# Batches in every eighth row of a quadrant, one transfer for the rows, and merged VectorE copies

## The chip, the cores and the metric

The kernel runs on one core of a Trainium2 chip. The metric is the device time of one execution in microseconds, as the median of several runs. TensorE, VectorE, ScalarE and GpSimd compute; SyncE issues nearly all transfers between HBM and the on-chip memory, which sixteen transfer engines carry out.

## The reference

One decoding step for four sequences (B = 4, one token each, D = 448): pre-LayerNorm, attention over the last 1024 positions of a cache with 16 query heads in 8 groups (head size 256), a residual, and then an MLP behind two further LayerNorms (D to 1792, GELU, back to 448) with biases and a residual. All in float32.

```python
def _A_ref(x, k_cache, v_cache, wq, wo):
    W = min(4096, max(256, Sk // 4))              # 1024
    q = (x @ wq).reshape(B, Sq, 16, 256).transpose(0, 2, 1, 3)
    k = repeat(k_cache[:, :, Sk - W:, :], 2, axis=1)
    v = repeat(v_cache[:, :, Sk - W:, :], 2, axis=1)
    p = softmax(einsum("bhqd,bhkd->bhqk", q, k) * 256 ** -0.5)
    return einsum("bhqk,bhkd->bhqd", p, v).transpose(0, 2, 1, 3).reshape(B, Sq, 4096) @ wo

def _B_ref(x, w1, b1, w2, b2):
    return gelu(layernorm(x) @ w1 + b1) @ w2 + b2

h = x + _A_ref(layernorm(x), k_cache, v_cache, wq, wo)
out = h + _B_ref(layernorm(h), w1, b1, w2, b2)
```

## The kernel before

The 128 partitions are used as four quadrants of Q = 32. In the attention a quadrant is a batch element, and the two query heads of a group are two of its 32 rows. Outside it, a quadrant is a fourth of the columns of x, and the four batch elements are four of its rows, the first four (rows 0 to 3, 32 to 35 and so on). TensorE works on four quadrants side by side: a matmul takes weights of 32 columns (or fewer, where only some rows are wanted) and writes to the partitions of its quadrant.

SyncE loads everything in an order written out by hand: `wq0` with x transposed, `k0`, two small pieces of `wq1`, and then in turn a block of k (with the projection weights of the next group but one) and a block of v (with its part of wo), 4992 KB each for most of the eight groups, two buffers for k and two for v (`load`, L48 to L54, all issued from L52). At the end v7 comes in four pieces, then `w1` in two and `w2` in three, in the buffers of k. The biases and rows of x come as `rows`, in four transfers of four rows on ScalarE's queue, one for each quadrant (L132), into the tile `rs`, which GpSimd clears first.

Each group g goes through `project_q` (L156: a projection, four transposes, a sum over the quadrants `sm`, two copies into `qT`), `scores` (L175: 32 matmul instructions, the row maximum `mx`, `nm` = -maximum x scale in two VectorE operations, the exponential), `transpose_p` (L203: eight transposes, four copies into `pT`), `values` (L216) and `transposed_output` with `add_output` (L234, L246). The scores of group g + 1 stand ahead of the values of group g. The order on TensorE is fixed as written (a manual schedule); the other engines' order is that of the scheduler.

After the last group comes a tail: group 7's output goes into `last`, the residual and the two LayerNorms follow (`h`, `d`, `z` and their sums through matmuls with `fold`), `z` is transposed by a matmul with `rows_of`, a selection of columns of the identity, into `zT`; `pu` (L388) multiplies it with w1, GELU gives `u`, which is transposed by `rows_of` (`put`, L407, L409) into `gT` (L411 on VectorE, L414 on ScalarE), and w2 is applied in two parts: `pa` (L421, chunks 0 to 7, copied out as `pas`) and `py` (L431, chunks 8 to 13, with `pas` added by L256). The sum with `hb` is stored as 128 rows of 512 bytes (L438). `keep_warm` issues matmuls without use for the clock. In `pu`, `pa` and `py` the first matmul of an accumulation takes weights of 32 columns, the others of four:

```python
m = Q if a == 0 else B
```

Of the kernel before, what the change touches and what calls it, by code (L numbers as in the profile page):

```python
# [11 lines left out]
ALU = mybir.AluOpType  # L12
# [3 lines left out]
B, D = 4, 448  # L16
HQ, HKV, SK, DH = 16, 8, 4096, 256
REP = HQ // HKV
W = min(4096, max(256, SK // 4))
F = 1792  # L20
P = 128
H = P // 2
ND = 4
NKC = W // P
NFC = F // P
FQ = F // 4
Q = 32
CACHE = NKC * B * DH
WEIGHTS = 4 * D
EPS = 1e-5  # L30
SCALE = DH ** -0.5

@with_exitstack
def block_kernel(ctx: ExitStack, tc, rows, wq0, k0, wq1, kq, vo, w1, w2, out):
    nc = tc.nc
# [30 lines left out]
    def load_k(g):  # L66
        half = CACHE // 2
        if g == 0:
# [3 lines left out]
            for i in range(2):  # L72
                nc.sync.dma_start(
                    wq1_last[i * Q : (i + 1) * Q, :], wq1[i].rearrange("e (p c) -> e p c", c=512)[:, :4, :]
                )
# [18 lines left out]
    ident = const.tile([P, P], F32, name="ident")  # L94
# [5 lines left out]

    sel = const.tile([P, Q], F32, name="sel")
    nc.vector.tensor_add(sel, ident[:, 0:Q], ident[:, Q : 2 * Q])
    nc.vector.tensor_add(sel, sel, ident[:, 2 * Q : 3 * Q])
    nc.vector.tensor_add(sel, sel, ident[:, 3 * Q : 4 * Q])


    yT = const.tile([P, ND + 1, Q], F32, name="yT")
    nc.vector.memset(yT, 0.0)
    wq1_last = const.tile([H, 512], F32, name="wq1_last")
    zT = const.tile([P, ND, Q], F32, name="zT")  # L110
# [5 lines left out]
        nc.vector.tensor_scalar_mul(fold[: 3 * Q, j, :], sel[: 3 * Q, :], 1.0 / D)  # L116
        nc.vector.tensor_scalar_mul(fold[3 * Q :, j, :], sel[3 * Q :, :], 0.5 / D)
    fold = fold.rearrange("p j q -> p (j q)")
    rows_of = ident.rearrange("p (j q) -> p j q", j=4)[:, :, :B]
    qT = [const.tile([P, 2, B, Q], F32, name=f"qT{i}") for i in range(2)]  # L120
    pT = [const.tile([P, NKC // 2, B, Q], F32, name=f"pT{i}") for i in range(2)]
    oT = [const.tile([P, 4, Q], F32, name=f"oT{i}") for i in range(2)]
    gT = const.tile([P, NFC, Q], F32, name="gT")
# [4 lines left out]

    rs = const.tile([P, 2 * P + FQ], F32, name="rs")
    nc.gpsimd.memset(rs, 0.0)  # L130
    for j in range(4):
        nc.scalar.dma_start(rs[j * Q : j * Q + B, :], rows[j])  # L132
    xb, b2b, b1b = rs[:, :P], rs[:, P : 2 * P], rs[:, 2 * P :]


# [20 lines left out]
    def project_q(g, parts):  # L156
        pq = ps_m.tile([P, 512], F32, tag="m", name=f"pq{g}")
        for j, y, cols, w in parts:
            nc.tensor.matmul(pq[j * Q : (j + 1) * Q, cols], y, w, start=True, stop=True)  # L159
        qs = work.tile([P, 512], F32, tag="qs", name=f"qs{g}")  # L160
        nc.scalar.copy(qs, pq)  # L161

        pt = ps_m.tile([P, 2 * REP, P], F32, tag="m", name=f"pqt{g}")
        for i in range(2 * REP):
            nc.tensor.transpose(pt[:, i, :], qs[:, i * P : (i + 1) * P], ident)  # L165
        sm = work.tile([P, 2 * REP, B], F32, tag="sm", name=f"sm{g}")
        nc.vector.tensor_reduce(  # L167
            sm, pt.rearrange("p i (j q) -> p i q j", j=4)[:, :, :B, :], axis=AX.X, op=ALU.add
        )

        src = sm.rearrange("p (r c) b -> p c b r", r=REP)
        for i in range(2):
            nc.vector.tensor_copy(qT[g % 2][:, :, :, i * REP : (i + 1) * REP], src)

    def scores(g, kt):  # L175
        mx = work.tile([P, 2], F32, tag="mx", name=f"mx{g}")
        halves = []
        for h in range(2):
            s = ps_s.tile([P, 512], F32, tag="s", name=f"s{g}_{h}")
            for c in range(2):  # L180
                for b in range(B):
                    nc.tensor.matmul(  # L182
                        s[b * Q : (b + 1) * Q, :], qT[g % 2][:, c, b, :], kt[h][:, c, b, :],
                        start=(c == 0), stop=(c == 1),
                    )
            nc.vector.reduce_max(mx[:, h : h + 1], s, axis=AX.X)  # L186
            halves.append(s)
        nm = work.tile([P, 1], F32, tag="nm", name=f"nm{g}")
        nc.vector.tensor_max(nm, mx[:, 0:1], mx[:, 1:2])
        nc.vector.tensor_scalar_mul(nm, nm, -SCALE)  # L190
        p = work.tile([P, 2 * 512], F32, tag="p", name=f"p{g}")
        sums = work.tile([P, 2], F32, tag="sums", name=f"sums{g}")
        for h in range(2):
            nc.scalar.activation(  # L194
                p[:, h * 512 : (h + 1) * 512], halves[h], AF.Exp, bias=nm, scale=SCALE,
                accum_out=sums[:, h : h + 1],
            )
        rec = work.tile([P, 1], F32, tag="rec", name=f"rec{g}")
        nc.vector.tensor_add(rec, sums[:, 0:1], sums[:, 1:2])
        nc.vector.reciprocal(rec, rec)  # L200
        return p, rec

    def transpose_p(g, p):  # L203
        for h in range(2):
            pt = ps_t.tile([P, 4, P], F32, tag="t", name=f"ppt{g}_{h}")
            for c in range(4):
                nc.tensor.transpose(pt[:, c, :], p[:, (4 * h + c) * P : (4 * h + c + 1) * P], ident)  # L207

            src = pt.rearrange("p (c i) (b q) -> p c i b q", i=2, b=B)
            for i in range(2):  # L210
                nc.vector.tensor_copy(  # L211
                    pT[g % 2][:, 2 * h : 2 * h + 2, :, i * REP : (i + 1) * REP], src[:, :, i, :, :REP]
                )


    def values(g, vt, po, pairs=range(NKC // 2)):  # L216
# [17 lines left out]
    def transposed_output(g, po, rec):  # L234
        o = work.tile([P, 2, DH], F32, tag="o", name=f"o{g}")
        nc.vector.tensor_scalar_mul(o, po, rec)  # L236
        pt = ps_m.tile([P, 2, 2, P], F32, tag="m", name=f"pot{g}")
        for i in range(2):
            for c in range(2):
                nc.tensor.transpose(pt[:, i, c], o[:, i, c * P : (c + 1) * P], ident)  # L240
        dst = oT[g % 2].rearrange("p (r c) q -> p c r q", r=REP)[:, :, :, :B]
        src = pt.rearrange("p i c (b q) -> p i c q b", b=B)
        nc.vector.tensor_copy(dst, src[:, 0, :, :REP])  # L243
        nc.vector.tensor_add(dst, dst, src[:, 1, :, REP : 2 * REP])  # L244
# [32 lines left out]
    p, rec = scores(0, kt)  # L277
    project_q(1, wqt)
    transpose_p(0, p)
    for g in range(HKV - 2):  # L280
        kt, wqt = load_k(g + 1)
        vt, wot = load_v(g)
        p, rec_next = scores(g + 1, kt)
# [9 lines left out]
    g = HKV - 2  # L293
# [5 lines left out]
    t = load("k", w2, (8 * D, 4 * D, 2 * D), "w2")  # L299
    w2t = [t[:, c * D : (c + 1) * D] for c in range(NFC)]  # L300
    p, rec_last = scores(g + 1, kt)


# [29 lines left out]
    for i in range(4):  # L333
        for j in range(4):
            nc.tensor.matmul(
                ph[j * Q : (j + 1) * Q], oT[(g + 1) % 2][:, i, :], columns(wo_last[:, i, :], j),
                start=False, stop=(i == 3),
# [18 lines left out]
    h = once.tile([P, P], F32, tag="h", name="h")  # L356
# [3 lines left out]
    m = row_mean(hs, pm[:, 0:1], "m")  # L360
# [4 lines left out]
    m = row_mean(ds, pm2[:, 0:1], "m2")  # L365
# [5 lines left out]
    nc.scalar.activation(junk, z, AF.Square, accum_out=zv)  # L371
    pz = ps_m.tile([P, 4, B], F32, tag="m", name="pz")
    nc.tensor.matmul(pz, z, rows_of, start=True, stop=True)
    nc.vector.tensor_copy(zT[:, :, :B], pz)
    hb = once.tile([P, P], F32, tag="hb", name="hb")
    nc.vector.tensor_add(hb, h, b2b)
    keep_warm(1, warm)
# [4 lines left out]
    pu = ps_s.tile([P, 512], F32, tag="s", name="pu")[:, :FQ]  # L382
    pv = ps_m.tile([P, 2], F32, tag="m", name="pv")
    for a in range(ND):
        m = Q if a == 0 else B
        for j in range(4):
            rows, w = w1_part(a, j)
            nc.tensor.matmul(  # L388
                pu[j * Q : j * Q + m, :], zT[rows, a, :m], w, start=(a == 0), stop=(a == ND - 1),
            )  # L390
        if a == 0:
            rsqrt(r1, row_mean(dv, pv[:, 0:1], "v1"), "r1")
        if a == 1:
            v2 = stat("v2")
            nc.vector.tensor_scalar(v2, row_mean(zv, pv[:, 1:2], "v2"), r1, r1, op0=ALU.mult, op1=ALU.mult)
            rsqrt(s, v2, "r2")
            nc.vector.tensor_mul(s, s, r1)
# [7 lines left out]
    put = ps_m.tile([P, 4, 4, B], F32, tag="m", name="put")  # L405
# [2 lines left out]
    for rows in (slice(0, H), slice(H, P)):  # L408
        nc.tensor.matmul(put[rows, 3], u[:, 3 * P :], rows_of, start=True, stop=True)  # L409
    dst = gT[:, :12, :].rearrange("p (c j) q -> p c j q", c=3)  # L410
    nc.vector.tensor_copy(dst[:, :, :, :B], put[:, :3])  # L411

    for i, rows in enumerate((slice(0, H), slice(H, P))):
        nc.scalar.copy(gT[rows, 12:, :B], put[rows, 3].rearrange("p (j i) q -> p j i q", i=2)[:, :, i, :])  # L414
    keep_warm(1, warm)

    first = 8
    pa = ps_w.tile([P, D], F32, tag="acc", name="pa")
    for c in range(first):
        j, m = c % 4, Q if c < 4 else B  # L420
        nc.tensor.matmul(  # L421
            pa[j * Q : j * Q + m, :], gT[:, c, :m], w2t[c], start=(c < 4), stop=(c >= first - 4),
        )
    pas = once.tile([P, D], F32, tag="u", name="pas")
    nc.scalar.copy(pas, pa)
    py = ps_o.tile([P, 2, H], F32, tag="o", name="py")
    for c in range(first, NFC):
        for j in range(4):
            m, n = (Q, 2) if c == first else (B, 2 if j < 3 else 1)
            w = columns(w2t[c], j) if n == 2 else w2t[c][:, None, 3 * P :]  # L430
            nc.tensor.matmul(  # L431
                py[j * Q : j * Q + m, :n, :], gT[:, c, :m], w, start=(c == first), stop=(c == NFC - 1),
            )
        if c == first + 1:
            add_quadrants(py, pas, False)
# [69 lines left out]
```

## Time and profile before

| | before |
|---|---|
| median of 3 runs | 214.59 us (214.52 to 214.6) |
| profiled execution, first to last instruction | 212.9 us |
| median less that span | 1.7 us |
| TensorE busy | 137.9 us (65%), 971 matmul instructions |
| VectorE busy | 39.2 us (18%), 167 instructions |
| ScalarE busy | 21.0 us (10%), 52 instructions |
| moved by transfers | 88.46 MB, 415 GB/s over the span |

The span is that of one profiled execution, which has no other time of its own; the difference to the median lies outside the first and the last instruction. Busy time says how long an engine worked, not whether anyone waited for it. A transfer is spread over several of the sixteen transfer engines and is complete when the slowest of them is.

### The profile page before, as it was taken

To read this page: it belongs to the slowest core of one execution; us is meant where nothing else is said; L and a number is where in the kernel's file an instruction comes from. 1 tells how busy PE (TensorE), PEld (TensorE's weight loads), DVE (VectorE), ACT (ScalarE), POOL (GpSimd) and SP (SyncE) were. 2 spreads that over 40 slices of the span, in tenths; PEclk is the share of its full clock that TensorE was granted. 3 is DMA by queue.
4 is the path that set the end of the run, shared out by engine and by line. 5 is a ranking of instruction groups with operands and counts; after the bars stand their busy time and mean duration, and the time that the engine had idled before them with its cause. 6 is when DMAs were issued, how large, how long until landed. Compare 5 with 4: busy or idle time off the path is not lost.

```text
span 212.9 us, 2306 instructions
## 1 busy us (share of the span) xinstructions
PE 137.9 (65%) x971; PEld 49.1 (23%) x971; DVE 39.2 (18%) x167; ACT 21.0 (10%) x52; POOL 5.6 (3%) x17
## 2 busy tenths in 40 slices
PE   0456868093886739583986348382948476798994
PEld 0322233021231212211231113120222123234432
DVE  1420324001130202210130104110230231022320
ACT  0210213000030000300030003000030001000311
POOL 6100000000000000000000000000000000000110
PEclk9999999669597966969599859979797999699999
DMA  7999998999989999999999999999989999999991
GB/s 291 426 399 469 398 465 378 459 465 390 458 378 465 465 390 458 398 446 465 390 458 405 443 465 386 465 413 428 461 375 468 440 428 390 417 418 433 424 390 60
DMA packets 3865, 88.46 MB, mean 415 GB/s; under 512 B 448, under 2 KB 576, under 8 KB 1168
## 3 DMA queue, kind: packets, MB, share of 16 engines
q1 hardware_dynamic: 3824, 88.29, 96.9%
q8 instruction: 7, 0.11, 0.2%
q10 hardware_dynamic: 32, 0.05, 0.1%
q14 instruction: 2, 0.02, 0.0%
HBM read 88.26 MB, written 0.07 MB: 415 GB/s over the span
## 4 chain that ended last, share of the span: by engine, by line
DMA 85%; PE 11%; DVE 2%; issue 0%; SPq 0%
DMA v<-vo 65%; DMA w<-w 12%; DMA k<-k 8%; PE po L219 8%; PE acc L248 1%; DVE o L236 1%; PE pot L240 1%; PE py L431 1%; DVE oT L243 0%; DVE oT L244 0%; SPq L52 0%; DVE res L437 0%; PE py L256 0%
## 5 line engine op out<-in xcount | busy, mean ns | idle before, releaser
L182 PE MATMUL s<-k,qT 128*32 128x512 f32 x256 | 42.3, 822 | 24.7 <-DMA k<-kq 22.6
L219 PE MATMUL po<-v,pT 128*32 128x512 f32 x256 | 40.0, 772 | 19.6 <-DMA v<-vo 19.6
L186 DVE TENSOR_REDUCE mx<-s 128x1 f32<-128x512 f32 x16 | 11.1, 691 | 67.4 <-PE s L182 67.4
L182 PEld LDWEIGHTS s<-k,qT 128*32 128x32 f32 x256 | 10.0, 146 | 54.7 <-issue 29.4
L219 PEld LDWEIGHTS po<-v,pT 128*32 128x32 f32 x256 | 10.7, 135 | 42.3 <-issue 31.4
L161 ACT COPY qs<-pq 128x512 f32<-128x512 f32 x8 | 4.7, 586 | 135.8 <-PE pq L159 135.8
L236 DVE TENSOR_SCALAR o<-po,rec 128x512 f32<-128x512 f32 x8 | 6.0, 750 | 60.2 <-PE po L219 60.2
L194 ACT ACTIVATE p<-s,nm 128x512 f32<-128x512 f32 x16 | 10.9, 690 | 18.4 <-DVE nm L190 18.4
L207 PE MATMUL ppt<-ident,p 128*128 128x128 f32 x64 | 10.5, 286 | 2.0 <-ACT p L194 1.7
L165 PE MATMUL pqt<-ident,qs 128*128 128x128 f32 x32 | 5.7, 304 | 6.2 <-ACT qs L161 6.2
L240 PE MATMUL pot<-ident,o 128*128 128x128 f32 x32 | 5.2, 286 | 5.7 <-DVE o L236 5.7
L248 PE MATMUL acc<-v,oT 128*32 128x448 f32 x56 | 6.7, 551 | 3.3 <-DVE oT L244 3.3
L207 PEld LDWEIGHTS ppt<-ident,p 128*128 128x128 f32 x64 | 6.7, 140 | 6.0 <-ACT p L194 6.0
L159 PE MATMUL pq<-k,yT 128*32 128x512 f32 (+1 forms) x66 | 7.3, 515 | 0.0
L308 PE MATMUL warm<-idle 128*32 128x512 bf16 x25 | 7.3, 382 | 0.0
L240 PEld LDWEIGHTS pot<-ident,o 128*128 128x128 f32 x32 | 3.3, 140 | 13.0 <-DVE o L236 13.0
L165 PEld LDWEIGHTS pqt<-ident,qs 128*128 128x128 f32 x32 | 3.6, 150 | 10.9 <-ACT qs L161 9.1
L153 POOL TENSOR_TENSOR r<-ve_r,mhalf 128x1 f32<-128x1 f32 x2 | 1.1, 544 | 191.9 <-DVE ve_r L152 191.9
L211 DVE COPY pT<-ppt 128x16 f32<-128x16 f32 x32 | 4.7, 170 | 4.7 <-PE ppt L207 4.7
L159 PEld LDWEIGHTS pq<-k,yT 128*32 128x32 f32 x66 | 3.1, 110 | 6.1 <-issue 4.8
L138 PE MATMUL pm_x<-wq,mean 128*128 128x12 f32 x2 | 0.6, 363 | 5.8 <-DMA wq<-wq 5.8
L167 DVE TENSOR_REDUCE sm<-pqt 128x16 f32<-128x64 f32 x8 | 1.8, 225 | 13.0 <-PE pqt L165 13.0
(101 smaller groups left out, 60.9 us busy)
## 6 DMA issues: line engine op xcount, KB each, us to landing
v<-vo SPq DMA_DIRECT2D x7, 4992.0 KB, 31.8
k<-kq SPq DMA_DIRECT2D x6, 4992.0 KB, 32.0
k<-k SPq DMA_DIRECT2D x1, 4864.0 KB, 16.3
k<-kq SPq DMA_DIRECT2D x1, 4096.0 KB
w<-w SPq DMA_DIRECT2D x2, 1792.0 KB
v<-vo SPq DMA_DIRECT2D x2, 1024.0 KB, 22.2
v<-vo SPq DMA_DIRECT2D x1, 2048.0 KB
w<-w SPq DMA_DIRECT2D x1, 1344.0 KB
```

The lines of the kernel that those rows point to most:

```text
L159: nc.tensor.matmul(pq[j * Q : (j + 1) * Q, cols], y, w, start=True, stop=True)
L161: nc.scalar.copy(qs, pq)
L165: nc.tensor.transpose(pt[:, i, :], qs[:, i * P : (i + 1) * P], ident)
L182: nc.tensor.matmul(s[b * Q : (b + 1) * Q, :], qT[g % 2][:, c, b, :], kt[h][:, c, b, :], start=(c == 0), stop=(c == 1),)
L186: nc.vector.reduce_max(mx[:, h : h + 1], s, axis=AX.X)
L194: nc.scalar.activation(p[:, h * 512 : (h + 1) * 512], halves[h], AF.Exp, bias=nm, scale=SCALE, accum_out=sums[:, h : h + 1],)
L207: nc.tensor.transpose(pt[:, c, :], p[:, (4 * h + c) * P : (4 * h + c + 1) * P], ident)
L219: nc.tensor.matmul(po[b * Q : (b + 1) * Q], pT[g % 2][:, c, b, :], vt[c][:, :, b, :], start=(c == 0), stop=(c == NKC // 2 - 1),)
L236: nc.vector.tensor_scalar_mul(o, po, rec)
L240: nc.tensor.transpose(pt[:, i, c], o[:, i, c * P : (c + 1) * P], ident)
L248: nc.tensor.matmul(acc[i * Q : (i + 1) * Q, :], oT[g % 2][:, i, :], wt[:, i, :], start=(g == 0), stop=(g == HKV - 2),)
L308: nc.tensor.matmul(warm[:Q], idle[:, :Q], idle, start=True, stop=True)
```

## The change

A batch element's row in a quadrant is now every eighth one (rows 0, 8, 16, 24 of 32; STEP = Q // B = 8) instead of the first four. So the sixteen rows of x and of the biases lie at partitions 0, 8, ..., 120, and one transfer of sixteen rows brings them. `rows_of` picks every eighth column of the identity; `oT`, `zT` and `gT` are written with a step of eight, and the matmuls of `pu`, `pa` and `py` take weights of 32 columns throughout, so that their outputs fill whole quadrants. The store itself has the same shape as before; the host picks other rows of it.

Apart from that, pairs of VectorE operations become single ones: the two copies into `qT` (8 fewer), two of the four copies into `pT` (16 fewer), and the two operations of `nm` (8 fewer), 32 in all.

```diff
-    rows_of = ident.rearrange("p (j q) -> p j q", j=4)[:, :, :B]
+    rows_of = ident.rearrange("p (j q) -> p j q", j=4)[:, :, ::STEP]
...
-    for j in range(4):
-        nc.scalar.dma_start(rs[j * Q : j * Q + B, :], rows[j])
+    nc.scalar.dma_start(rs[::STEP, :], rows)
...
-        src = sm.rearrange("p (r c) b -> p c b r", r=REP)
-        for i in range(2):
-            nc.vector.tensor_copy(qT[g % 2][:, :, :, i * REP : (i + 1) * REP], src)
+        src = sm.rearrange("p (r c) b -> p c b r", r=REP)[:, :, :, None, :].to_broadcast([P, 2, B, 2, REP])
+        nc.vector.tensor_copy(qT[g % 2][:, :, :, : 2 * REP].rearrange("p c b (i r) -> p c b i r", i=2), src)
...
-        nc.vector.tensor_max(nm, mx[:, 0:1], mx[:, 1:2])
-        nc.vector.tensor_scalar_mul(nm, nm, -SCALE)
+        nc.vector.tensor_scalar(nm, mx[:, 0:1], mx[:, 1:2], -SCALE, op0=ALU.max, op1=ALU.mult)
...
-            src = pt.rearrange("p (c i) (b q) -> p c i b q", i=2, b=B)
-            for i in range(2):
-                nc.vector.tensor_copy(
-                    pT[g % 2][:, 2 * h : 2 * h + 2, :, i * REP : (i + 1) * REP], src[:, :, i, :, :REP]
-                )
+            src = pt.rearrange("p (c i) (b q) -> p c b i q", i=2, b=B)[:, :, :, :, :REP]
+            dst = pT[g % 2][:, 2 * h : 2 * h + 2, :, : 2 * REP]
+            nc.vector.tensor_copy(dst.rearrange("p c b (i r) -> p c b i r", i=2), src)
...
-        dst = oT[g % 2].rearrange("p (r c) q -> p c r q", r=REP)[:, :, :, :B]
+        dst = oT[g % 2].rearrange("p (r c) q -> p c r q", r=REP)[:, :, :, ::STEP]
...
-    nc.vector.tensor_copy(zT[:, :, :B], pz)
+    nc.vector.tensor_copy(zT[:, :, ::STEP], pz)
...
-        m = Q if a == 0 else B
...
-                pu[j * Q : j * Q + m, :], zT[rows, a, :m], w, start=(a == 0), stop=(a == ND - 1),
+                pu[j * Q : (j + 1) * Q, :], zT[rows, a, :], w, start=(a == 0), stop=(a == ND - 1),
...
-            pa[j * Q : j * Q + m, :], gT[:, c, :m], w2t[c], start=(c < 4), stop=(c >= first - 4),
+            pa[j * Q : (j + 1) * Q, :], gT[:, c, :], w2t[c], start=(c < 4), stop=(c >= first - 4),
...
-            m, n = (Q, 2) if c == first else (B, 2 if j < 3 else 1)
+            n = 2 if c == first or j < 3 else 1
...
-                py[j * Q : j * Q + m, :n, :], gT[:, c, :m], w, start=(c == first), stop=(c == NFC - 1),
+                py[j * Q : (j + 1) * Q, :n, :], gT[:, c, :], w, start=(c == first), stop=(c == NFC - 1),
```

The writes of `gT` (L411, L414) get the step of eight in the same way.

More of the change, by code (lines that the diff above doesn't have):

```diff
@@ L27 @@
 Q = 32
+STEP = Q // B
 CACHE = NKC * B * DH
@@ L410, in block_kernel @@
     dst = gT[:, :12, :].rearrange("p (c j) q -> p c j q", c=3)
-    nc.vector.tensor_copy(dst[:, :, :, :B], put[:, :3])
+    nc.vector.tensor_copy(dst[:, :, :, ::STEP], put[:, :3])
     for i, rows in enumerate((slice(0, H), slice(H, P))):
-        nc.scalar.copy(gT[rows, 12:, :B], put[rows, 3].rearrange("p (j i) q -> p j i q", i=2)[:, :, i, :])
+        nc.scalar.copy(gT[rows, 12:, ::STEP], put[rows, 3].rearrange("p (j i) q -> p j i q", i=2)[:, :, i, :])
     keep_warm(1, warm)
@@ L419, in block_kernel @@
     for c in range(first):
-        j, m = c % 4, Q if c < 4 else B
+        j = c % 4
         nc.tensor.matmul(
-            pa[j * Q : j * Q + m, :], gT[:, c, :m], w2t[c], start=(c < 4), stop=(c >= first - 4),
+            pa[j * Q : (j + 1) * Q, :], gT[:, c, :], w2t[c], start=(c < 4), stop=(c >= first - 4),
         )
@@ L488 @@
     rows = np.concatenate([quadrants(xp), quadrants(b2), quadrants(np.asarray(B_b1).reshape(1, F))], axis=2)
+    rows = rows.reshape(4 * B, 2 * P + FQ)
     arrays = {
@@ L502 @@
     r = run(nc, [arrays], core_ids=[0])
-    got = np.asarray(r.results[0]["out"]).reshape(4, Q, P)[:, :B, :]
+    got = np.asarray(r.results[0]["out"]).reshape(4, B, STEP, P)[:, :, 0]
     return np.ascontiguousarray(got.transpose(1, 0, 2).reshape(B, 1, 4 * P)[:, :, :D])
```

## The prediction

> **What bounds the kernel now.** I read the page's header and slices first, then its queues and its chain. Columns of a queue row: packets, MB, time of those packets as a share of what 16 transfer engines have in the span.
>
> ```profile
> span 212.9 us, 2306 instructions
> DMA  7999998999989999999999999999989999999991
> ...
> q1 hardware_dynamic: 3824, 88.29, 96.9%
> q8 instruction: 7, 0.11, 0.2%
> q10 hardware_dynamic: 32, 0.05, 0.1%
> ...
> HBM read 88.26 MB, written 0.07 MB: 415 GB/s over the span
> ```
>
> SyncE's queue (q1) fills 96.9% of the engines' time, and no slice between the first and the last falls under 80%. 88.29 MB have to pass, so the end of the stream sets the end unless something starves it. Two views say whether anything can: the issues (KB each, median us from issue to landing) and what SyncE waited for (us, times, longest).
>
> ```profile
> v<-vo SPq DMA_DIRECT2D x7, 4992.0 KB, 31.8
> k<-kq SPq DMA_DIRECT2D x6, 4992.0 KB, 32.0
> ...
> rs<-rows ACTq DMA_DIRECT2D x4, 11.0 KB
> ```
> ```profile
> SPq L52 <- PE acc L248: 48.7, 6, 8.5
> SPq L52 <- PE pq L159: 39.0, 6, 7.5
> ...
> SPq L52 <- DMA k<-k: 11.4, 1, 11.4
> ```
>
> A block of 4992 KB takes 4992 x 1024 B / 415 GB/s = 12.3 us, but it lands 32 us after its issue: 32 - 12.3, about 20 us of it, is queueing behind earlier blocks. SyncE's waits for a free buffer (`acc`, `pq`) last at most 8.5 us and end with those 20 us still queued. An earlier release changes an issue time, not a transfer. The chain on the page, which alternates transfers with TensorE's work, follows buffer releases and hides this.
>
> The second place is the end: the timeline (start, us busy, what, [idle before <-releaser]) and the stretches (us, PE busy (x), PEld, DVE, ACT, POOL, PEclk, DMA share, GB/s).
>
> ```profile
> 207.49 0.55 PE L421 MATMUL pa<-w,gT 128*4 128x448 f32 x3
> 208.15 0.53 ACT L425 COPY pas<-pa 128x448 f32<-128x448 f32 x1 [1.62 <-PE pa L421]
> ...
> 208.41 0.64 PE L431 MATMUL py<-w,gT 128*32 128x128 f32 x16 [0.37 <-DMA w<-w]
> ...
> 208.78 0.48 PE L256 MATMUL py<-pas,sel 128*32 128x128 f32 x8
> ...
> 209.00 1.14 PE L431 MATMUL py<-w,gT 128*4 128x64 f32 x32
> 210.21 0.29 DVE L437 TENSOR_TENSOR res<-py,hb 128x128 f32<-128x128 f32 x1 [4.05 <-PE py L431]
> ```
> ```profile
> 206.50:207.00 0.50, 0.50 (x8) 0.13 (x4) 0.00 (x0) 0.03 (x1) 0.00 (x0) 1.00 0.92 380
> 207.00:207.50 0.50, 0.50 (x12) 0.13 (x4) 0.00 (x0) 0.00 (x0) 0.00 (x0) 1.00 0.75 308
> 207.50:208.00 0.50, 0.50 (x8) 0.00 (x0) 0.00 (x0) 0.00 (x0) 0.00 (x0) 1.00 0.61 244
> 208.00:208.50 0.50, 0.13 (x7) 0.09 (x8) 0.00 (x0) 0.35 (x1) 0.00 (x0) 1.00 0.60 244
> 208.50:209.00 0.50, 0.50 (x24) 0.50 (x28) 0.00 (x0) 0.18 (x1) 0.00 (x0) 1.00 0.17 65
> ```
>
> TensorE is done with `pa` at 207.49 + 0.55 = 208.04, waits 0.37 us for a piece of w2, and then works without a gap to 210.14. The end has two covers: 0.37 us in front of `py`, and between the end of `pas` (208.15 + 0.53 = 208.68) and L256, which reads it (208.78), 0.10 us. And the transfer engines do not end together: from 207.5 to 208.5 the share is 0.60, ten of sixteen at work, six finished a full us earlier. A load counts as landed when the slowest engine is through, so what matters is which engines carry more.
>
> **The change part by part.** The 32 VectorE instructions:
>
> ```profile
> L211 DVE COPY pT<-ppt 128x16 f32<-128x16 f32 x32 | 4.7, 170 | 4.7 <-PE ppt L207 4.7
> ...
> L173 DVE COPY qT<-sm 128x16 f32<-128x16 f32 x16 | 2.0, 172 | 0.3
> ...
> L189 DVE TENSOR_TENSOR nm<-mx 128x1 f32<-128x1 f32 x8 | 1.3, 159 | 0.3
> ...
> L190 DVE TENSOR_SCALAR nm<-nm 128x1 f32<-128x1 f32 x8 | 1.2, 154 | 0.3
> ...
> L411 DVE COPY gT<-put 128x48 f32<-128x48 f32 x1 | 0.2, 208 | 1.3 <-PE put L409 1.3
> ...
> L374 DVE COPY zT<-pz 128x16 f32<-128x16 f32 x1 | 0.2, 175 | 0.5 <-PE pz L373 0.5
> ```
>
> A pair of copies of 16 elements (2 x 170 ns) becomes one of 32. Its price lies between 172 (16 elements) and 208 ns (48), so I take 190: 16 in `transpose_p` save 16 x (340 - 190) = 2.4 us, 8 in `project_q` 8 x (344 - 190) = 1.2, and the 8 of `nm` 8 x about 0.15 = 1.2. That makes 4.8 us of VectorE. All of it lies in the eight groups before the last `v` block; nothing in the tail is merged. The cover is the 20 us queue, and SyncE's release comes from `pq` and `acc`, which stand before the merged copies or on a chain (L236, L243, L244) that keeps its instructions. Worth 0. With the cover gone it would be 4.8 / 8 = 0.6 us a group.
>
> Writing every eighth row: `qT` and `pT` are already written in runs of two values, and those copies take 170 and 172 ns against 175 for `zT`, which is written in runs of four. Single values should cost the same, bounds -5 to +10 ns on five operations of the tail (two on `oT`, one on `zT`, one on `gT`, the pair on ScalarE): +0.02 us, hidden by the covers. `rows_of` as a moving operand with a step of eight has no row before it; eight matmuls of 16 columns read it. If each cost as much as 128 columns instead of 16, that is 273 - 266 ns:
>
> ```profile
> L407 PE MATMUL put<-ident,u 128*128 128x16 f32 x6 | 0.8, 266 | 0.4 <-ACT u L402 0.4
> ...
> L431 PE MATMUL py<-w,gT 128*4 128x128 f32 x30 | 1.4, 273 | 0.0
> ```
>
> 8 x 7 ns = 0.06 us, again under the cover. I take 0.
>
> Weights of 32 columns instead of 4 (`pu` from a = 1, `pa` from c = 4, `py` from c = 9):
>
> ```profile
> L388 PEld LDWEIGHTS pu<-w,zT 128*32 128x32 f32 x8 | 0.2, 108 | 0.2 <-DVE zT L374 0.2
> ...
> L388 PEld LDWEIGHTS pu<-w,zT 128*4 128x4 f32 x16 | 0.2, 84 | 0.0
> ...
> L388 PEld LDWEIGHTS pu<-w,zT 64*4 64x4 f32 x8 | 0.1, 80 | 0.8 <-issue 0.8
> ...
> L421 PEld LDWEIGHTS pa<-w,gT 128*4 128x4 f32 x8 | 0.3, 86 | 0.5 <-issue 0.5
> ...
> L431 PEld LDWEIGHTS py<-w,gT 128*4 128x4 f32 x40 | 1.1, 86 | 0.1
> ```
>
> 108 - 85, some 23 ns a load, on 72 loads. They run beside the matmuls of the previous tile; only the first load of a run that starts cold shows: two in `pu` (behind `pv`) and one in `py` where the last piece of w2 arrives. 2 x 23 ns vanish in the 0.37 us; one, 0.02 us, stays on the path.
>
> The rows. Queue q10 shows 32 packets for 16 rows of 11.0 / 4 = 2.75 KB: 16 of data and 16 small ones, four to a transfer, which I read as the end marks of four engines. So four engines carry four rows each and twelve carry none. A row takes 2816 B / (415 / 16 GB/s) = 0.109 us of an engine. After: if sixteen engines take one row each, the four lose 3 x 0.109 = 0.33 us and the twelve gain 0.109. The Trainium skill ("DMA: Bandwidth & Descriptors", section "Why a DMA increments its semaphore by 16 and not by 1") says the same: the number of engines is the largest up to 16 that divides the slowest dimension, so 4 for four rows and 16 for sixteen. The small packets bear out the four; no row here shows the sixteen.
>
> Which engines end last? Ten are late, by a good us, so the four alone don't make the late group. What costs an engine that much is an instruction packet: 0.2% x 16 x 212.9 us / 7 = 1.0 us each, seven of them. I therefore put the last engine among those seven, without rows until now: +0.11 us on the stream, bounds -0.33 and +0.11. Fewer issues on ScalarE's queue (four down to one, in the first 6 us) free nothing that anyone waits for; and SyncE's 11.4 us wait for k0, which ends with k0's landing although the buffer of the next block was never used, may go, but a block issued earlier still queues behind k0 and k1.
>
> Sum against the profiled span: 212.9 + 0.11 + 0.02 = 213.03 us. The median of the runs, 214.59, has 1.7 us outside the span, untouched: 214.7 us. A difference under 0.2% (0.43 us) is about what a measurement of this kernel can't tell from none.
>
> **The rivals.** *The four row engines decide the end.* Then the stream ends 0.33 us earlier; `py` may start at 208.08, still after `pa`, but L256 waits for `pas`, and only the 0.10 us cover is gained: 214.5 us, and 214.3 if the tail follows fully. Against it: ten late engines, not four.
>
> *The wide weight loads stand in the path* (the other side). Place: the 72 loads of the tail; point: as soon as a load can't run ahead of the matmuls before it. Price 72 x 23 ns = 1.66 us, less the 0.37 us cover: 1.3 us, 214.7 + 1.3 = 216.0 us. The Trainium skill ("TensorE: Matmul & The Clock Gate", section "LDWEIGHTS (loading the stationary operand)") has load time grow with the columns, so the rule speaks against this change; by its 1/1.2 ns a column, 28 more columns are an estimated 23 ns, as in the rows. Against it, a row with the same 32 instructions and wide weights:
>
> ```profile
> 195.78 1.08 PE L335 MATMUL last<-v,oT 128*32 128x128 f32 x32 [0.15 <-DVE oT L244]
> ```
>
> It needs 1.08 us, the narrow `py` 1.14.
>
> *The rows do not go to sixteen engines* (the change doesn't do what it says). All sixteen on one engine are 16 x 0.109 = 1.74 us, 1.3 more than a row engine has now; an engine of the early six has a us of cover, one of the ten has none: 214.9 to 216.0 us.
>
> *The VectorE saving reaches the path.* With 0.6 us a group for perhaps three of the eight groups: 1.8 us, 212.9 us. It needs an empty transfer queue, and the slices show none.
>
> **How the numbers follow.** Forecast 0.64, row engines 0.16, weight loads 0.07, rows on few engines 0.06, VectorE 0.07. The first two make 0.80 and span 214.3 to 214.7; unknown small costs of the tail, the covers used up (0.06 + 0.02 + 2 x 0.02 + another 0.29 should an operation such as L437's move into the tail's path), reach 215.1. So 214.3 to 215.1. Faster by over 0.2%: 0.07 of the VectorE case and 0.01 of the row engines', 0.08. Slower: 0.07 + 0.06 and 0.03 of the forecast's own upper end, 0.16. Same: the rest of the forecast and of the row engines, 0.61 + 0.15 = 0.76.
>
> **What would show it.** Right: q10 again with 32 packets but one issue; q1 unchanged; 135 VectorE instructions instead of 167 and some 34 us busy; `py` still started by a transfer, at 208.4 to 208.6; L388, L421 and L431 with 32 columns and the same matmul times. Wrong: a wait in front of L431 that is gone (the loads or the tail took over), q10 with 17 packets (one engine), or the stream's last slices draining in another shape, with fewer late engines.

## The result and the profile after

The changed kernel takes 214.94 us (median of 21 runs, 214.8 to 215.19); the kernel before takes 214.55 us (21 runs on the same chip, 214.36 to 215.02). The ratio is 1.0018, 95% interval 1.0012 to 1.0024: 0.39 us slower by the medians, 0.26 to 0.51 us by the interval. The profiled execution of the changed kernel has a span of 213.2 us and belongs to a run of 214.98 us; the part outside the span is 1.8 us in both kernels. The profile of the kernel before, with a span of 212.9 us, therefore belongs to an execution of some 214.7 us, 0.16 us above its median.

The page of the changed kernel (header, engines, slices, queues):

```profile
span 213.2 us, 2269 instructions
PE 135.3 (63%) x971; PEld 48.0 (22%) x971; DVE 37.4 (18%) x135; ACT 21.0 (10%) x52; POOL 5.6 (3%) x17
...
DMA  7999998998989989999899998999989998999981
...
q1 hardware_dynamic: 3824, 88.29, 96.8%
q8 instruction: 7, 0.11, 0.2%
q10 hardware_dynamic: 32, 0.05, 0.1%
```

SyncE's queue still fills the transfer engines, 96.8% against 96.9%. The bytes and packets are the same, the row packets too (32, now from one issue). VectorE has the 135 instructions of the forecast.

The tail of the changed kernel, in the timeline's columns (start, us busy, what, [idle before <-releaser]):

```profile
208.25 0.53 ACT L420 COPY pas<-pa 128x448 f32<-128x448 f32 x1 [1.59 <-PE pa L416]
...
208.51 0.64 PE L426 MATMUL py<-w,gT 128*32 128x128 f32 x16 [0.36 <-DMA w<-w]
208.88 0.48 PE L252 MATMUL py<-pas,sel 128*32 128x128 f32 x8
...
209.10 1.13 PE L426 MATMUL py<-w,gT 128*32 128x64 f32 x32
210.31 0.29 DVE L432 TENSOR_TENSOR res<-py,hb 128x128 f32<-128x128 f32 x1 [4.03 <-PE py L426]
210.63 0.35 SPq L433 DMA_DIRECT2D out<-res  x1
```

`py`, which waits for a piece of w2, starts at 208.51, before at 208.41: in these two executions the stream ends 0.10 us later. From there to `res` it is 1.80 us in both kernels (208.41 to 210.21, 208.51 to 210.31). So 0.10 of the 0.3 us by which the spans differ is there when the store is issued, and the other 0.2 us comes after it. By the medians the first part is larger: 0.39 less the 0.18 found below is 0.21 us, since the profile before is of a longer execution than its median.

After the store SyncE only waits. The view of what SyncE waited for (us, times, longest) has that wait, first in the kernel before, then in the changed one. It counts from the check ahead of it, so the two numbers are not the store's own time:

```profile
SPq L499 <- DMA out<-res: 0.9, 1, 0.9
```
```profile
SPq L495 <- DMA out<-res: 1.1, 1, 1.1
```

The views group SyncE's last instructions, so here they are one by one from the records of the two traces: eight transfer counters are used in turn by the kernel's transfers, and at the end SyncE checks them in a fixed order, in five steps.

```
start, us                     before    after
issue of the store            210.533   210.629
checks done before it         210.932, 211.001, 211.063, 211.127   211.028
check that the store ends     212.103   212.191
checks behind it              none      212.252, 212.317, 212.378
drain                         212.168   212.443
issue of the store to drain     1.635     1.814
```

Both stores are through 1.56 to 1.57 us after their issue. Before, the store is transfer 32 and its counter is the last in the order. Now it is transfer 29, its counter stands second, and three more checks of some 0.063 us each (0.061 to 0.065) stand behind it: 1.814 - 1.635 = 0.18 us. (The plain three checks are 3 x 0.063 = 0.19.) The four row transfers that became one moved the store's place in this order.

### The profile page after: what moved, and what is told of

It is laid out like the page before. It is cut to its first block, busy times and chain, and to the rows that moved or that the text cites. A ratio compares the mean times of both kernels' runs of the same rounds, so it can differ in the third digit from the quotient of the medians.

```text
span 213.2 us, 2269 instructions
## 1 busy us (share of the span) xinstructions
PE 135.3 (63%) x971; PEld 48.0 (22%) x971; DVE 37.4 (18%) x135; ACT 21.0 (10%) x52; POOL 5.6 (3%) x17
## 3 DMA queue, kind: packets, MB, share of 16 engines
q1 hardware_dynamic: 3824, 88.29, 96.8%
## 4 chain that ended last, share of the span: by engine, by line
DMA 84%; PE 11%; DVE 2%; SPq 1%; issue 1%
DMA v<-vo 72%; DMA w<-w 12%; PE po L215 8%; PE acc L244 1%; DVE o L232 1%; PE pot L236 1%; PE py L426 1%; SPq L74 1%; SPq L53 1%; DVE oT L239 0%; DVE oT L240 0%; DVE res L432 0%; PE py L252 0%
## 5 line engine op out<-in xcount | busy, mean ns | idle before, releaser
L215 PE MATMUL po<-v,pT 128*32 128x512 f32 x256 | 36.0, 710 | 21.4 <-DMA v<-vo 21.4
L215 PEld LDWEIGHTS po<-v,pT 128*32 128x32 f32 x256 | 9.0, 127 | 42.6 <-issue 29.4
L383 PE MATMUL pu<-w,zT 128*32 128x448 f32 (+1 forms) x32 | 3.8, 550 | 0.4 <-DMA w<-w 0.4
## 6 DMA issues: line engine op xcount, KB each, us to landing
k<-k SPq DMA_DIRECT2D x1, 4864.0 KB, 16.3
```

Of the source, the lines that this page charges most:

```text
L215: nc.tensor.matmul(po[b * Q : (b + 1) * Q], pT[g % 2][:, c, b, :], vt[c][:, :, b, :], start=(c == 0), stop=(c == NKC // 2 - 1),)
```

## The experiments

Each kernel ran beside the kernel before on the same chip; "over" is the difference of medians to it.

**e1_four_rows**: the changed kernel with the rows in four transfers again.

```diff
-    nc.scalar.dma_start(rs[::STEP, :], rows)
+    for j in range(4):
+        nc.scalar.dma_start(rs[j * Q : (j + 1) * Q : STEP, :], rows[j * B : (j + 1) * B, :])
```


> The changed kernel with the rows of x and biases again in four transfers of four rows; every eighth row, wide weights and merged copies stay. Theory A: the +0.39 us of the change comes from the rows transfer alone, about 0.1 us because each of the sixteen transfer engines now carries a row, and about 0.19 us because the store of the result has become the second instead of the last thing that SyncE checks at the end (three more checks of 0.063 us behind it). Then this kernel is at before: py starts at 208.37 plus or minus 0.05, span 212.9, time within 0.1 us of before. Theory B: the wide weights and the steps of eight in the tail cost it. Then it stays 0.2 to 0.4 us over before, with py's start or the stretch from py to the store longer.

Measured: 214.72 us (11 runs, before 214.55), ratio 1.0011, interval 1.0002 to 1.0020. Its close is that of the kernel before, with the store checked last (1.63 us from issue to drain), so by subtraction all of the 0.17 us lies in the stream. (Its profile is of one of its fastest runs, 214.59 us, and can't show it.) Three of the runs lay at 215.05 to 215.16, the median of the others is 0.15 us above the kernel before. With the rows on four engines again, the stream did not come back.

**e2_four_columns**: sixteen rows in each of four transfers of a quarter of the columns, so that sixteen engines carry rows, and 32 transfers are issued.

```diff
-    nc.scalar.dma_start(rs[::STEP, :], rows)
+    n = (2 * P + FQ) // 4
+    for j in range(4):
+        nc.scalar.dma_start(rs[::STEP, j * n : (j + 1) * n], rows[:, j * n : (j + 1) * n])
```


> The changed kernel with the sixteen rows in four transfers of sixteen rows and 176 columns each: all sixteen engines carry as many bytes as in the changed kernel, but the number of transfers is that of before, so the store should be checked last again. Theory A: py starts as in the changed kernel (208.46, 0.1 us over before), but the close behind the store is 0.19 us shorter: time 0.10 to 0.20 us over before. Rival (transfer engines alone cost the 0.39 us): as slow as the changed kernel, 0.35 to 0.40 over before.

Measured: 214.71 us (11 runs), ratio 1.001, interval 1.0001 to 1.0019: 0.16 us over the kernel before, 0.23 under the changed one. Its rows queue on the page and its wait for the store:

```profile
q10 hardware_dynamic: 128, 0.05, 0.1%
```
```profile
SPq L497 <- DMA out<-res: 0.9, 1, 0.9
```

128 packets are 4 x (16 pieces of rows + 16 end marks): a transfer of sixteen rows does go to sixteen engines, as the prediction read from the Trainium skill ("DMA: Bandwidth & Descriptors", section "Why a DMA increments its semaphore by 16 and not by 1"); e1's four transfers of four rows show 32, that is 4 x (4 + 4). The wait is 0.9 again. The changed kernel's close without its three checks gives 214.94 - 0.19 = 214.75, which is e2 to within 0.04.

**e3_merges_only**: the kernel before with the three merges alone.

```diff
-        nc.vector.tensor_max(nm, mx[:, 0:1], mx[:, 1:2])
-        nc.vector.tensor_scalar_mul(nm, nm, -SCALE)
+        nc.vector.tensor_scalar(nm, mx[:, 0:1], mx[:, 1:2], -SCALE, op0=ALU.max, op1=ALU.mult)
...
```


> The kernel before with the merged VectorE copies alone (32 instructions fewer), first four rows, four transfers. Prediction's reading: nothing of it reaches the end, since the transfer queue is never empty: within 0.1 us of before, VectorE busy 1.8 us less as in the changed kernel, py starting at 208.37 plus or minus 0.05. Rival (VectorE on the path): 0.3 us or more faster, the end of the w blocks earlier.

Measured: 214.53 us (11 runs, before 214.55), ratio 1.0, interval 0.9991 to 1.0009. The merges are worth nothing that these runs can show; the interval is 0.2 us to either side.

**e4_one_more_small**: the kernel before with a 33rd transfer, of 4 rows of 16 bytes, never read.

```diff
+    extra = const.tile([P, B], F32, name="extra")
+    nc.scalar.dma_start(extra[:B, :], rows[0][:, :B])
```


> The kernel before with one more transfer of four rows of 16 bytes behind the four row transfers, of no weight for the engines; the copy is never read. Theory A on the close: with one transfer more the store moves on by one place and becomes the first thing that SyncE checks at the end, so four checks of 0.063 us come behind it instead of none: 0.25 us over before, all of it behind the store's landing, py's start unchanged at 208.37. Rival (the order of checks is no matter): within 0.06 us of before.

Measured: 214.66 us (11 runs), ratio 1.0005, interval 0.9996 to 1.0014: 0.11 us, not 0.25. The records show why: the store's counter stood third in the order, not first, with two checks behind it (211.879 and 211.941, drain 212.006). Two checks are 2 x 0.063 = 0.13 us, and from issue to drain it is 1.735 us, 0.10 more than before. The price of a check held, my place for the store was wrong. The 0.11 us of the runs fits the 0.10 of the close, though their interval alone still holds zero.

**e5_wide_weights**: the kernel before with weights of 32 columns in `pu`, `pa` and `py`.

```diff
-        m = Q if a == 0 else B
+        m = Q
...
-        j, m = c % 4, Q if c < 4 else B
+        j, m = c % 4, Q
...
-            m, n = (Q, 2) if c == first else (B, 2 if j < 3 else 1)
+            m, n = (Q, 2) if c == first else (Q, 2 if j < 3 else 1)
```


> The kernel before with weights of 32 columns in pu, pa and py (the added rows of zT and gT are zero), nothing else changed. The prediction's working: one load of 23 ns on the path, so within 0.1 us of before. Theory B (the wide weights are what keeps the changed kernel with four row transfers at 214.72): 0.13 to 0.24 us over before, and the stretch from py's first matmul to the store no longer 1.80 us, or py no longer started by a transfer.

Measured: 214.54 us (11 runs, before 214.51), ratio 1.0001, interval 0.9992 to 1.001. Its group of loads and its tail:

```profile
L431 PEld LDWEIGHTS py<-w,gT 128*32 128x32 f32 x48 | 1.3, 109 | 1.2 <-DMA w<-w 1.1
```
```profile
208.21 0.64 PE L431 MATMUL py<-w,gT 128*32 128x128 f32 x16 [0.33 <-DMA w<-w]
...
210.01 0.29 DVE L437 TENSOR_TENSOR res<-py,hb 128x128 f32<-128x128 f32 x1 [3.95 <-PE py L431]
```

Every load takes 109 ns instead of 86, and from `py` to `res` it is 1.80 us as before. The loads lie beside the matmuls.

**e6_layout_only**: e1 with the merges undone, that is the layout alone with four row transfers.

```diff
-        nc.vector.tensor_scalar(nm, mx[:, 0:1], mx[:, 1:2], -SCALE, op0=ALU.max, op1=ALU.mult)
+        nc.vector.tensor_max(nm, mx[:, 0:1], mx[:, 1:2])
+        nc.vector.tensor_scalar_mul(nm, nm, -SCALE)
...
```


> The changed kernel with four row transfers and without the merged copies: what is left is the layout, every eighth row with the steps and the wide weights. Theory A: within 0.1 us of before, and the 0.17 us of the four-row kernel is spread between its runs. Theory B: 0.13 to 0.24 us over before again, as the merged copies alone gave 0.0.

Measured: 214.84 us (11 runs, before 214.51), ratio 1.0014, interval 1.0005 to 1.0023. `py` still waits for its transfer:

```profile
208.39 0.64 PE L431 MATMUL py<-w,gT 128*32 128x128 f32 x16 [0.38 <-DMA w<-w]
```
```profile
4.07 3.02 ACTq L133 DMA_DIRECT2D rs<-rows  x4
```

So 0.3 us comes with the layout, by subtraction in the stream, since the store is checked last here too. The second line is new: the four issues with a step take ScalarE's queue 3.02 us, against 1.54 us in the kernel before.

**e7_wide_rows_four** and **e8_wide_rows_one** ask what bytes in the rows cost: the kernel before with rows twice as long on the same four engines, and the changed kernel with rows four times as long on sixteen. What is added is never read.

```diff
-    rs = const.tile([P, 2 * P + FQ], F32, name="rs")
+    rs = const.tile([P, 2 * (2 * P + FQ)], F32, name="rs")
...
+    rows = np.concatenate([rows, rows], axis=2)
```


> The kernel before with every row of the four row transfers twice as long (the second half is a copy that is never read): the four engines that carry rows get 4 x 0.109 = 0.44 us more, the other twelve nothing. Prediction's reading, the four are not the last: 0.0 to 0.1 us over before. Rival (the four row engines decide the end): 0.44 us over before, py's start at 208.8.

```diff
-    rs = const.tile([P, 2 * P + FQ], F32, name="rs")
+    rs = const.tile([P, 4 * (2 * P + FQ)], F32, name="rs")
...
+    rows = np.concatenate([rows] * 4, axis=1)
```


> The changed kernel with every one of the sixteen rows four times as long (three copies are never read), still one transfer: each of the sixteen engines gets 3 x 0.109 = 0.33 us more. Theory A: the last engine is later by that, 0.33 us over the changed kernel and 0.65 to 0.75 over before (215.2 to 215.3 us), py's start at 208.8. Rival (bytes on single engines don't matter, the total does): 132 KB more at 415 GB/s are the same 0.33 us; but then the kernel with wide rows on four engines is 44 KB, 0.11 us, over before whatever engines carry them.

Measured: e7 215.74 us (5 runs, before 214.51), ratio 1.0056, interval 1.0044 to 1.0069; e8 215.73 us (5 runs), ratio 1.0061, interval 1.0048 to 1.0074. Both theories missed both, by far: 1.2 us for e7 where at most 0.44 was expected. The first long block, k0, shows it in the issues, first e7, then e8 (before and after have 16.3 us there):

```profile
k<-k SPq DMA_DIRECT2D x1, 4864.0 KB, 17.9
```
```profile
k<-k SPq DMA_DIRECT2D x1, 4864.0 KB, 17.8
```

In the records of e8 a row takes 422 to 806 ns of its engine (four times 112 would be 448), and thirteen packets of k0 beside the rows take 2.01 to 2.37 us instead of 1.44. So in e8 a long row costs its engine more than its bytes. In e7 a row takes 215 to 229 ns, twice the 112 of before as its bytes would have it, and only one packet of k0 exceeds 2 us; where its 1.2 us come from is open. Both kernels also have a wider `rs`, which shifts the tiles behind it in the on-chip memory; a wider tile without the bytes was not tried, so neither run prices the bytes alone.

**e9_store_last**: the changed kernel with three small transfers more, 32 in all.

```diff
+    extra = const.tile([P, 3 * B], F32, name="extra")
+    for i in range(3):
+        nc.scalar.dma_start(extra[:B, i * B : (i + 1) * B], rows[:B, i * B : (i + 1) * B])
```


> The changed kernel with three more transfers of 4 rows of 16 bytes (never read) behind the rows, 32 transfers in all as before the change, so that the store's counter should again be the last that SyncE checks. Theory of the close: three checks of 0.063 us behind the store go, 0.19 us under the changed kernel, about 214.75 us, the start of py unchanged within 0.05 us. Rival (all of the loss is in the stream): no gain, or a little loss from three more issues, 214.9 to 215.0 us.

Measured: 214.99 us (12 runs, before 214.54), ratio 1.0025, interval 1.0013 to 1.0037: the number that the rival gave. Its wait for the store and one of its stretches:

```profile
SPq L498 <- DMA out<-res: 0.9, 1, 0.9
```
```profile
207.50:208.00 0.50, 0.50 (x8) 0.22 (x4) 0.00 (x0) 0.00 (x0) 0.00 (x0) 0.50 0.70 280
```

The store is checked last, and from its issue to the drain it is 1.618 us, 0.20 less than in the changed kernel. So the checks did go, and the time did not: by subtraction about as much was lost elsewhere. In this profile the last packet of the loads ends at 209.45 us, in the changed kernel's at 209.07, so the stream is later. But it is the profile of the longest execution, 216.52 us, in which TensorE's granted clock in the tail was 0.50 (the other eleven lie at 214.81 to 215.16). e9 shows the price of the close by its records, and leaves its effect on the time unconfirmed.

**e10_rows_late, e11_four_rows_late, e12_before_rows_late**: the changed kernel, e1 and the kernel before, each with its row transfers written into the third pass of the group loop, to get them away from the first blocks. In the changed kernel:

```diff
-    nc.scalar.dma_start(rs[::STEP, :], rows)
...
+        if g == 2:
+            nc.scalar.dma_start(rs[::STEP, :], rows)
```


> The changed kernel with the transfer of the 16 rows issued in the third pass of the group loop (some 87 us) instead of at the start. Theory that a row costs its engine its own bytes wherever it falls: the same as the changed kernel within 0.05 us, 214.9 us. Rival (the rows cost what they disturb among the first blocks, k0 and k1): the stream ends 0.1 to 0.2 us earlier, 214.7 to 214.8 us. The close stays as in the changed kernel, store second.

> The changed kernel with the rows in four transfers of 4 rows at step 8 (as in e1_four_rows), issued in the third pass of the group loop. If what e1 and e6 lost against the kernel before comes from the moment at which these rows meet the first blocks: 214.5 us, no difference from the kernel before. If it comes from which engines carry the rows or from the stepped writes themselves: 214.7 to 214.85 us as in e1 and e6.

> The kernel before with its four row transfers issued in the third pass of the group loop. Control: both theories say no difference from the kernel before, 214.5 us within 0.05, since four engines with rows do not decide the end there; if the rows did delay the first blocks, up to 0.1 us less.

Measured, 11 runs each, before 214.54: e10 214.88 us (ratio 1.0013, interval 1.0005 to 1.0022), e11 214.75 (1.0009, 1.0001 to 1.0018), e12 214.56 (1.0002, 0.9993 to 1.0011). But the transfers did not move. Their issues in e10, then in e11, then in e12:

```profile
4.07 0.57 ACTq L286 DMA_DIRECT2D rs<-rows  x1
```
```profile
4.07 2.43 ACTq L287 DMA_DIRECT2D rs<-rows  x3
13.50 0.58 ACTq L287 DMA_DIRECT2D rs<-rows  x1
```
```profile
4.07 1.19 ACTq L290 DMA_DIRECT2D rs<-rows  x3
13.39 0.26 ACTq L290 DMA_DIRECT2D rs<-rows  x1
```

The order on ScalarE is the scheduler's, and it put the issue back to 4.07 us, where it stands in the changed kernel and in the kernel before; of four transfers only the last came later, at 13.5 and 13.4 us instead of 6.5 and 5.3, and still beside the first blocks. So these runs say nothing of the moment of the rows, and none of the three expectations was put to the test. What they are is a repetition: e10 of the changed kernel (0.34 us over before; the changed kernel 0.39), e11 nearly of e1 (0.21; e1 0.17), e12 nearly of the kernel before (0.02).

**All of them together.** Less what each profile has in the close over that of the kernel before (0.18 us in the changed kernel and e10, 0.10 in e4, nothing in the others), the stream's share of each median over the kernel before is:

| | rows on | us |
|---|---|---|
| changed kernel, e10, e2 | sixteen engines | 0.21, 0.16, 0.16 |
| e1, e11, e6 (every eighth row) | four engines | 0.17, 0.21, 0.33 |
| e3, e4, e5, e12 (first four rows) | four engines | -0.02, 0.01, 0.03, 0.02 |

One median is uncertain by 0.13 to 0.2 us, but the kernels fall into two groups by the layout, and not by the number of engines that carry rows. e9, with the layout and three transfers more, stands outside at 0.45.

## Why the prediction was right, and where

The forecast was 214.7 us and most of its chance (0.76) lay on a difference too small to tell, under 0.2% (0.43 us); it came out as 214.94, inside 214.3 to 215.1, 0.18% slower, and with 21 runs each that can be told from none. The direction and the size are right, the way there only in part, and some of it is luck: the sum has 0.13 us, the loss is 0.39, of which 0.18 comes from a place that the sum left out and about 0.2 from the stream, for a reason that the runs do not bear out. The range had its upper end from costs in the tail, and those did not come: from `py` to `res` it is 1.80 us in both. By its steps:

**The stream bounds the kernel, the merges are worth 0: right, shown by e3.** The saving itself was mis-sized: VectorE's busy time fell from 39.2 to 37.4 us, by 1.8, where I had summed 4.8 and expected some 34 us. The timeline of the two kernels has one pair and what it became:

```profile
86.86 0.25 DVE L173 COPY qT<-sm 128x16 f32<-128x16 f32 x2
```
```profile
85.94 0.18 DVE L172 COPY qT<-sm 128x32 f32<-128x32 f32 x1
```

I had charged the pair with 2 x 172 = 344 ns; two copies in a row overlap and take 0.25 us together. My price of 190 ns for the merged copy was good:

```profile
L209 DVE COPY pT<-ppt 128x32 f32<-128x32 f32 x16 | 3.1, 191 | 5.0 <-PE ppt L205 5.0
...
L188 DVE TENSOR_SCALAR nm<-mx 128x1 f32<-128x1 f32 x8 | 1.7, 214 | 0.3
L239 DVE COPY oT<-pot 128x16 f32<-128x16 f32 x8 | 1.5, 186 | 6.0 <-PE pot L236 6.0
...
L406 DVE COPY gT<-put 128x48 f32<-128x48 f32 x1 | 0.2, 244 | 1.3 <-PE put L404 1.3
```

The merged `nm` takes 214 ns and not 154; the groups' own times show the overlap (the row quoted before gives 32 copies 4.7 us, which is less than 32 x 170 ns).

**Stepped writes: priced too low, hidden all the same.** `oT` rose from 174 to 186 ns, `zT` from 175 to 186 and `gT` from 208 to 244, outside my bounds of -5 to +10 ns. The row of `oT` before:

```profile
L243 DVE COPY oT<-pot 128x16 f32<-128x16 f32 x8 | 1.4, 174 | 6.0 <-PE pot L240 6.0
```

`py` still waits 0.36 us for its transfer, so the cover holds those in the tail.

**Wide weights: right, shown by e5.** 109 against 86 ns a load, and no time. The rival of 216.0 us is out, and with it what the Trainium skill's load time would have made of it ("TensorE: Matmul & The Clock Gate", section "LDWEIGHTS (loading the stationary operand)"): the loads do grow with the columns as it says, but no matmul waits for them.

**The rows on sixteen engines: right, shown by the 128 packets of e2. That they cost the stream 0.11 us: not borne out.** The stream's share of the loss is what is left without the close, 0.26 to 0.51 less 0.18, so 0.08 to 0.33 us, 0.21 by the medians. The term lies within that, but e1, e6 and e11 keep the rows on four engines and lose 0.17, 0.33 and 0.21 us. What they share with the changed kernel is the layout; the merges (e3) and the wide weights (e5) are excluded. Which part of the layout delays the stream is open: the stepped writes of VectorE and ScalarE, the stepped row transfers, or the array of rows with sixteen rows in place of four times four; when the row transfers are issued was not varied.

One of the prediction's own signs of being wrong did show: fewer late engines. Eight of sixteen are still at work from 207.5 us, not ten, and more of them after 208.5 (the shares were 0.61 and 0.17):

```profile
207.50:208.00 0.50, 0.50 (x8) 0.00 (x0) 0.00 (x0) 0.00 (x0) 0.00 (x0) 1.00 0.50 201
...
208.50:209.00 0.50, 0.49 (x21) 0.49 (x25) 0.00 (x0) 0.29 (x1) 0.00 (x0) 1.00 0.29 115
```

In that stretch from 207.5 us the share is 0.52 in e2 and 0.64 in e1, so the rows seem to decide how many engines are late, and not when the last one ends. My reading of the late group, engines hit by instruction packets, is in part borne out: in the records of both kernels the seven instruction packets take 0.94 to 1.13 us (1.0 as I had it), and the data packet behind one takes about 0.5 us more, for example 1.94 to 1.98 us instead of 1.48. The records do not name the engines, so that the one that ends last is among these seven is not shown.

**SyncE's wait for k0 may go, worth nothing: the worth is right, and another wait took its place.** SyncE's issues of the first blocks, in the kernel before and in the changed one:

```profile
5.68 0.34 SPq L52 DMA_DIRECT2D k<-kq  x1
17.46 0.33 SPq L52 DMA_DIRECT2D v<-vo  x1
24.29 0.33 SPq L52 DMA_DIRECT2D k<-kq  x1
```
```profile
3.22 0.44 SPq L53 DMA_DIRECT2D k<-kq  x1
3.71 0.45 SPq L53 DMA_DIRECT2D v<-vo  x1
25.06 0.33 SPq L53 DMA_DIRECT2D k<-kq  x1
```

v0 is issued 13.75 us earlier, a wait for k0 (now 13.3 us) stands behind it instead of ahead of it, and the next block is issued at about the same time, 25.06 against 24.29 us. All of them queue behind k0 and k1, and the end does not gain. Why the wait stood there before is in the records: v0 was the tenth transfer, and with eight counters in turn it had to use that of the second, k0, and waited until k0 had landed. In the changed kernel v0 is issued as the sixth and finds a free one; the wait for k0 there stands ahead of the third block of k, which goes into the buffer of k0. It is the same turn of counters that moved the store's check.

**"1.7 us outside the span untouched": right (1.8 in both), but the sum stopped too early.** It let the span end with the stream and `res`. Between the store's issue and the drain lies SyncE's own close, and fewer transfers made that longer by 0.18 us, nearly half of the whole loss. I had counted the four issues that became one only by what they free on ScalarE's queue. The sum that the traces bear out is 214.55 + 0.18 (close) + 0.1 to 0.2 (stream) = 214.8 to 214.9, with the median of the changed kernel's runs at 214.94. Of the two terms the close is read from the records of the two kernels; the stream's is what is left, located in the layout and not explained.

## What to carry to other kernels

Where a transfer stream sets the end, as here, time saved on an engine was worth nothing, and a layout is judged by what it does to the stream and to what comes after the stream. Follow the last store to the final drain in the sum, too: SyncE's checks behind it are part of the span, and in this kernel the number of transfers decided how many there were. When a loss of 0.2% is to be explained, undo the parts one by one before believing the first mechanism that has the right size. And read in the trace whether an experiment's edit arrived: the rows that were written into the third pass were issued at 4.07 us all the same.

## What was not expected of the hardware

- SyncE checks the transfer counters at the end in a fixed order, in five steps of some 0.063 us each. The store's place in it moved with the number of transfers: last with 32, third with 33, second with 29.
- Four row transfers with a step of eight rows take ScalarE's queue 3.02 us to issue, 1.54 us without a step, and one transfer of sixteen rows 0.57 us.
- Kernels with rows of 5.6 KB (e7) or 11.3 KB (e8) instead of 2.8 KB, in a wider tile, took 1.2 us more; beside the rows of 11.3 KB thirteen packets took 2.01 to 2.37 us instead of 1.44.
- A data packet behind one of the seven instruction packets took about 0.5 us more than its like.
- With eight counters in turn, a transfer waits for the one eight places ahead of it: v0 was issued at 17.46 us as the tenth transfer and at 3.71 us as the sixth.
- Two short VectorE copies in a row overlap: 0.25 us for a pair of 0.17 us each.
